# A fourth tile for the values of an attention stage, loaded at other places of the plan, and half the ring for GpSimd's transfers

## The chip, the cores and the metric

The kernel runs on one core of a Trainium2 chip. The metric is the device time of one execution in microseconds (us). A core has five engines with instruction streams of their own: TensorE (PE; its weight loads are shown apart as PEld), VectorE (DVE), ScalarE (ACT), GpSimd (POOL) and SyncE (SP). Each stream runs in order. SP computes nothing here: it issues nearly all transfers, and a transfer that has to wait holds everything behind it on SP. POOL issues some stores of the second half of the kernel.

## The reference, cut to what matters

Attention over 8 batches, 12 heads, 448 tokens and 64 elements per head, with the heads mixed by a 12x12 matrix before and another after the softmax; then a feed-forward layer on the 3584 x 768 result. Everything is float32.

```python
scores = scale * np.matmul(q, k.transpose(0, 1, 3, 2))
scores = np.einsum('bhij,hg->bgij', scores, w_pre)
scores = scores - np.max(scores, axis=-1, keepdims=True)
attn = np.exp(scores)
attn = attn / (np.sum(attn, axis=-1, keepdims=True) + 1e-09)
attn = np.einsum('bhij,hg->bgij', attn, w_post)
attn_out = np.matmul(attn, v)
# x: attn_out as [3584, 768]
h = x @ w_in            # 768 x 2048
g = h - np.tanh(h)
out = g @ w_out         # 2048 x 768
```

## The kernel before

**Two halves.** The attention stage takes the first 838 us or so of the span, the feed-forward stage the rest. [...]

**Blocks, groups, places.** Each batch has four blocks of query tokens (120, 120, 120 and 88). A block is cut into groups of ten tokens or fewer, so that ten tokens times twelve heads fill 120 partitions; a batch has 45 groups, all batches 360. Two groups make a *place*, the unit of the plan: 180 places (`NPL`), 22.5 to a batch. Place p does, in this order in the program:

- SP gathers the two groups of place p+2 (`gather`, L907: scores in SBUF, head-major, to rows of token and head, `t`), then sends what waits in two lists (`issue`, L769: at most six, the list of ordinary loads and stores ahead of the list of the weight conversion, each entry in a place after the one that asked for it);
- PE mixes the heads of place p (`premix`, L918, out of `t`, eight matmuls); DVE takes maxima (L927) and ACT exponentials (L929); DVE and POOL make the normalized second mixing matrix of place p-1 (`norm`, L936 to L938, `wr`);
- then come the jobs that the planner put at this place (`todo`): transposes of K (`prep_k`) and Q (`prep_q`), scores of a pair of heads for a later block (`scores`, L874), and attention times V for half the heads of an earlier block (`values`, L997);
- PE mixes place p-1 (`mix`, L955, 32 matmuls, needs `wr`), and DVE writes the result of `values` to a staging tile `x` (L1015). After every second block, and after the last of a batch, `x` is stored to DRAM (`xs`). There is one `x`, so the next write to it waits until that store has landed.

SP runs ahead of PE: what SP issues for place p goes out while PE is in p-1 or p, unless SP is held up.

**The weight conversion** (class `Convert`) runs through the attention stage as well: it loads a piece of the weights (`cr`), splits it on DVE, POOL and ACT, and stores the parts (`co` to `wi` or `wo`, `ct` to `ss` or `ts`). `co` has two buffers, so DVE's L88 and L94, which write into it, wait until an earlier store has landed. DVE being in order, all behind them waits too: `norm`, and so `mix` on PE.

**Values.** V of a batch comes in three loads of 448 KB (`load_v`, L784), hq = 0, 1, 2, each with four heads. The tag `vr` has three tiles, so load hq of batch b takes the tile of load hq of batch b-1. `values(i, 0)` reads loads 0 and 1, `values(i, 1)` reads 1 and 2. The loop at L1197 asks for load hq of batch b at place p0 + 4 + hq, where p0 is the first place of the batch; entries are sent in the next place. Loads of K (`load_k`, three per batch, 448 KB each in pieces of 256 B) and of Q (one per block) are asked for by the same planner.

**Names that the change touches:** `load_v` (L784) and its pool of tiles; the list `halved` and the loop that takes it apart (L1163 on), which fixes the place of each `values`; the loop at L1197; and the size of the ring at L1382.

Of the kernel before, what the change touches and what calls it, by code (L numbers as in the profile page):

```python
# [10 lines left out]
F32 = mybir.dt.float32  # L11
# [137 lines left out]
def kernel_body(  # L149
# [11 lines left out]
    nc = tc.nc  # L161
    B, H, S, D = q.shape
# [3 lines left out]
    NP = H // 2  # L166
    CP = 112
    NC = S // CP
# [567 lines left out]
    with ExitStack() as st:  # L736
# [7 lines left out]
        kp = st.enter_context(tc.tile_pool(name="kp", bufs=1, side="right"))  # L744
# [14 lines left out]
        def dma(dst, src, to=None):  # L759
            entry = [place[0], dst, src, None]  # L760
            (queue if to is None else to).append(entry)
            return lambda places=0: entry[3] is not None and entry[3] + places <= place[0]
# [19 lines left out]
            krs[b, hq] = t  # L782

        def load_v(b, hq):  # L784
            t = kp.tile([CP, 4, NC, D], F32, name="vr", tag="vr", bufs=3)
            sent[b, hq, "v"] = dma(
                t.rearrange("p h c d -> p h (c d)"),
                v[b, 4 * hq : 4 * hq + 4].rearrange("h (p c) d -> p h (c d)", c=NC),
            )
            vts[b, hq] = t  # L790
# [254 lines left out]
        for hq in range(3):  # L1045
            load_v(0, hq)
# [101 lines left out]
        def at_place(p, *job):  # L1148
            todo[p].append(job)

        halved = []
        for i in range(len(blocks)):
# [7 lines left out]
                    halved.append((e if i else x - 1, hi, "s", i + 1, x))  # L1160
            for x in range(2):
                halved.append(((f1 - 1) // 2 + 2, f2 // 2 + 1 if f2 < NG else NPL + 7, "v", i, x))
        at_s, p, kind = {}, 0, None  # L1163
        window = {i: (lo, hi) for lo, hi, k, i, _ in sorted(halved, reverse=True) if k == "s"}
        while halved:
            ready = sorted((x for x in halved if x[0] <= p), key=lambda x: (x[1], x[3:]))
            if ready:
                x = ready[0]
                assert p <= x[1], (p, x)

                other = [y for y in ready if y[2] != kind]
                if x[2] == kind and other and x[1] > p + 1:
                    x = other[0]
                halved.remove(x)
                _, _, kind, i, n = x
                if kind == "s":
                    at_s[i, n] = p
                    for hp in (2 * n, 2 * n + 1):
                        at_place(p, scores, i, hp)
                else:  # L1180
                    at_place(p, values, i, n)
            p += 1

# [2 lines left out]
        def held(p):  # L1186
            return [a for f, *a in todo[p] if f is scores]

        for p in range(1, NPL):
            if any(f in (scores, values) for f, *a in todo[p]):  # L1190
                continue
            for of, n in ((p - 1, 1), (p + 1, 0)):
                if len(held(of)) == 2 and window[held(of)[n][0]][0] <= p <= window[held(of)[n][0]][1]:
                    i, hp = held(of)[n]
# [4 lines left out]
        for i, (b, m) in enumerate(blocks):  # L1199
            p0 = first[i] // 2  # L1200
            if i + 2 < len(blocks):
                p = at_s[i + 2, 0] - 1
                at_place(p, prep_q, i + 2, 0)
                at_place(p, prep_q, i + 2, 1)
                if i + 3 < len(blocks):
                    at_place(p + 1, load_q, i + 3)
            if b and m == 0:
                for hq in range(NP // 2):
                    at_place(p0 + 4 + hq, load_v, b, hq)
        for b in range(1, B):  # L1210
            p, o, done = first[blocks.index((b - 1, 1))] // 2 - 4, 0, []
            for hq in range(3):
                if hq == 2:

                    p = max(p, done[0] + 1)
# [112 lines left out]
    for s in range(NS):  # L1328
# [24 lines left out]
        n = HELD[s] + AHEAD[s]  # L1353
# [44 lines left out]
```

## Time and profile before

| | |
|---|---|
| median of three runs | 1712.13 us (1706.76 to 1722.13) |
| the profiled execution, its own time | 1711.91 us |
| its span, first to last instruction | 1710.2 us |
| mean granted TensorE clock | 0.986 |
| busy share of the span: PE, PEld, DVE, ACT, POOL | 98%, 81%, 72%, 64%, 35% |
| instructions | 40889 |

The profile is of one execution. A busy PE is not PE at its peak, since matmuls overlap and their ends are modelled; what PE waits for is read from the waits, and how fast it ran from the granted clock (PEclk, 1.00 is full speed). A line of the timeline gives the start, the length, the engine, the line of the kernel, what is written and read, how many instructions were drawn together (x32), and in brackets the idle time of the engine before it with what ended it. A line of the windows gives a stretch, its length, the busy time and number of instructions of PE, PEld, DVE, ACT and POOL, then PEclk, the mean busy share of the 16 DMA engines, and GB/s.

### The profile page before, as it was taken

The page shows a single profiled execution, that of the slowest core. Times are in us where ns is not written, and L with a number is a line of the kernel's source. Part 1 is how long each engine was busy: PE and PEld are TensorE (multiplying, and loading weights), DVE is VectorE, ACT ScalarE, POOL GpSimd, SP SyncE. Part 2 cuts the span into 40 slices and gives each one's busy share as a digit, 9 for nine tenths or more (in the row PEclk, how much of TensorE's full clock was granted, in tenths as well). Part 3 has the DMA queues.
Part 4 walks back from the last instruction along what each step waited for, and adds up shares of the span by engine and source line. Part 5 has one row for each costly group of instructions (what it writes and reads, how often), then busy time and mean ns, then how long its engine had stood idle before and what let it go on. Part 6 is the DMA issues. An engine that isn't in the chain of part 4 may idle for free.

```text
span 1710.2 us, 40889 instructions
## 1 busy us (share of the span) xinstructions
PE 1668.2 (98%) x16068; PEld 1391.2 (81%) x16068; DVE 1238.5 (72%) x1939; ACT 1091.9 (64%) x1896; POOL 601.7 (35%) x798
## 2 busy tenths in 40 slices
PE   8999999999999999999999999999999999999999
PEld 6777777777777777777787888888888888889999
DVE  5776776868868788676488799858788868778432
ACT  4776776767767677677677677565667456665331
POOL 1566575666757667563100011101001101011100
PEclk9999999999999999999999999999999999999999
DMA  8779789787887988876579899988999989988993
GB/s 190 219 233 256 228 247 266 232 253 240 247 269 231 249 252 242 253 223 210 179 260 327 291 321 311 345 300 321 321 342 352 384 272 333 320 312 327 404 413 133
DMA packets 322286, 475.06 MB, mean 278 GB/s; under 512 B 105264, under 2 KB 255280, under 8 KB 322096
## 3 DMA queue, kind: packets, MB, share of 16 engines
q1 hardware_dynamic: 305660, 414.34, 74.9%
q0 software_dynamic: 16128, 57.68, 8.7%
q8 instruction: 128, 2.10, 0.5%
q14 instruction: 62, 0.51, 0.1%
q10 hardware_dynamic: 308, 0.43, 0.1%
HBM read 274.73 MB, written 120.59 MB: 231 GB/s over the span
## 4 chain that ended last, share of the span: by engine, by line
PE 82%; DMA 9%; DVE 4%; ACT 3%; issue 2%; SPq 1%; POOL 0%; ACTq 0%; DVEq 0%; POOLq 0%
PE ps_o L955 15%; PE ps_p L918 9%; PE ps_m L997 8%; PE ps_q L874 7%; PE ps_h L289 7%; PE ps_h L290 7%; PE ps_h L292 7%; PE y L530 6%; PE y L532 6%; PE y L531 6%; DMA gl<-gs 2%; DMA t<-s 2%; DMA vr<-in_v_dram 1%; PE ps_m L840 1%; DMA wi<-co 1%
## 5 line engine op out<-in xcount | busy, mean ns | idle before, releaser
L955 PEld LDWEIGHTS ps_o<-wr,e 60*112 60x112 f32 (+1 forms) x5760 | 310.1, 177 | 33.2 <-POOL wr L938 17.4
L955 PE MATMUL ps_o<-wr,e 60*112 60x60 f32 (+1 forms) x5760 | 317.8, 261 | 8.7 <-POOL wr L938 8.0
L929 ACT ACTIVATE e<-ps_p,mx 128x448 f32<-128x448 f32 x360 | 225.3, 631 | 114.6 <-DVE mx L927 76.2
L927 DVE TENSOR_REDUCE mx<-ps_p 128x1 f32<-128x448 f32 x360 | 206.6, 615 | 88.2 <-PE ps_p L918 87.7
L965 ACT COPY at<-ps_o 112x960 f32<-112x960 f32 x156 | 153.9, 986 | 116.1 <-PE ps_o L955 115.8
L918 PE MATMUL ps_p<-t,wpre 60*64 60x448 f32 (+1 forms) x1440 | 183.1, 576 | 9.5 <-DMA t<-s 7.6
L997 PEld LDWEIGHTS ps_m<-at,vr 112*64 112x64 f32 x3072 | 150.1, 138 | 29.6 <-issue 8.0
L997 PE MATMUL ps_m<-at,vr 112*64 112x120 f32 (+1 forms) x3072 | 164.3, 264 | 6.2 <-DMA vr<-in_v_dram 6.2
L938 POOL TENSOR_TENSOR wr<-wpost,zs 128x120 f32<-128x120 f32 x180 | 69.6, 387 | 286.4 <-DVE zs L937 221.2
L530 PE MATMUL y<-w,gh 128*128 128x384 f32 x448 | 151.1, 337 | 2.3 <-issue 0.8
L531 PE MATMUL y<-w,gh 128*128 128x384 f32 x448 | 150.3, 336 | 0.0
L532 PE MATMUL y<-w,gl 128*128 128x384 f32 x424 | 143.1, 337 | 2.0 <-DVE gl L448 2.0
L874 PEld LDWEIGHTS ps_q<-kk,qh 64*120 64x120 f32 (+1 forms) x768 | 60.4, 177 | 83.5 <-issue 43.0
L874 PE MATMUL ps_q<-kk,qh 64*120 64x448 f32 (+1 forms) x768 | 124.5, 401 | 1.2 <-DVE kk L826 0.5
L669 POOL DMA_DIRECT2D gs<-gb x24 | 17.2, 718 | 292.2 <-DVE gb L668 292.2
L879 DVE COPY s<-ps_q 120x448 f32<-120x448 f32 (+1 forms) x192 | 112.4, 614 | 8.7 <-PE ps_q L874 8.4
L305 ACT ACTIVATE u<-h 128x1024 f32<-128x1024 f32 x56 | 59.5, 1063 | 74.2 <-DVE h L716 70.2
L879 ACT COPY s<-ps_q 120x448 f32<-120x448 f32 (+1 forms) x192 | 95.0, 536 | 7.0 <-PE ps_q L874 6.7
L645 POOL DMA_DIRECT2D gs<-ga x24 | 17.2, 716 | 229.6 <-DVE ga L328 222.4
L530 PEld LDWEIGHTS y<-w,gh 128*128 128x128 f32 x448 | 84.1, 188 | 7.6 <-issue 2.1
L531 PEld LDWEIGHTS y<-w,gh 128*128 128x128 f32 x448 | 84.1, 188 | 3.4
L532 PEld LDWEIGHTS y<-w,gl 128*128 128x128 f32 x424 | 79.5, 188 | 3.0 <-DVE gl L448 3.0
(371 smaller groups left out, 3987.9 us busy)
## 6 DMA issues: line engine op xcount, KB each, us to landing
t<-s SPq DMA_DIRECT2D x342, 210.0 KB
wa<-ss SPq DMA_DIRECT2D x96, 384.0 KB
w<-wo SPq DMA_DIRECT2D x43, 768.0 KB
gl<-gs SPq DMA_DIRECT2D x62, 512.0 KB
wa<-wi SPq DMA_DIRECT2D x72, 384.0 KB
w<-ts SPq DMA_DIRECT2D x35, 768.0 KB
gs<-gs POOLq DMA_DIRECT2D x24, 768.0 KB, 9.1
cr<-in_moe_w_in_dram SPq DMA_DIRECT2D x48, 256.0 KB
```

Source lines behind the costliest of these rows:

```text
L289: nc.tensor.matmul(ph, w[:, c, 0], xh, start=start and c == 0, stop=False, skip_group_check=True)
L530: nc.tensor.matmul(y, gh[:, tok], wh, start=first, stop=False, skip_group_check=True)
L531: nc.tensor.matmul(y, gh[:, tok], wl, start=False, stop=False, skip_group_check=True)
L532: nc.tensor.matmul(y, gl[:, tok], wh, start=False, stop=last, skip_group_check=True)
L874: nc.tensor.matmul(ps[:n, :S], qx[a, hp, :], kx[a, hp % 2], start=(x == 0), stop=(x == 2))
L879: eng(sts[i][:n, 2 * hp + j, :], ps[:n, :S])
L918: nc.tensor.matmul(pss[r][halves[j], :], wpre[k, :], ts[j][k, :], start=True, stop=True)
L927: nc.vector.tensor_reduce(out=mx, in_=ps, axis=AX.X, op=ALU.max, negate=True)
L929: nc.scalar.activation(e, ps, AF.Exp, bias=mx, scale=1.0, accum_out=zs[:, 0, r : r + 1])
L955: nc.tensor.matmul(ps[:CP, j, c * GP : (c + 1) * GP].rearrange("p (h i) -> p h i", i=GI)[:, :, r * GH : (r + 1) * GH], e[k, c * CP : (c + ...
L965: nc.scalar.copy(ats[i0][:, :, :, at : at + 2 * GI].rearrange("p c h (j i) -> p j (c h) i", j=2), ps[:CP, :, : NC * GP].rearrange("p j (x ...
L997: nc.tensor.matmul(pv[j * D : (j + 1) * D, r, :n], vt[:, j, c, :], ats[i][:, c, 2 * hp + j, :n], start=(c == 0), stop=(c == NC - 1),)
```

## The change

Four tiles `vr` instead of three. The loads now take turns over four tiles: load hq of batch b takes the tile of the load four before it, so load 0 takes a tile whose last reader lies more than a batch back, load 1 that of load 0 of the batch before, load 2 that of load 1. Load 0 is asked for at p0 - 3, seven places sooner; load 1 at the place where `values(i-1, 0)` of the last block before stands, which is the last reader of its tile; load 2 at that of `values(i-1, 1)`. A dictionary `at_v` keeps these places. The ring for the descriptors of GpSimd's transfers shrinks from 4096 to 2048 bytes per partition; the fourth tile takes 4096.

```diff
         def load_v(b, hq):
-            t = kp.tile([CP, 4, NC, D], F32, name="vr", tag="vr", bufs=3)
+            t = kp.tile([CP, 4, NC, D], F32, name="vr", tag="vr", bufs=4)
...
-        at_s, p, kind = {}, 0, None
+        at_s, at_v, p, kind = {}, {}, 0, None
...
                 else:
+                    at_v[i, n] = p
                     at_place(p, values, i, n)
...
             if b and m == 0:
-                for hq in range(NP // 2):
-                    at_place(p0 + 4 + hq, load_v, b, hq)
+                at_place(p0 - 3, load_v, b, 0)
+                for hq in (1, 2):
+                    at_place(at_v[i - 1, hq - 1], load_v, b, hq)
...
-    nc = _bacc.Bacc("TRN2", target_bir_lowering=False, num_devices=1, dynamic_dma_scratch_size=4096)
+    nc = _bacc.Bacc("TRN2", target_bir_lowering=False, num_devices=1, dynamic_dma_scratch_size=2048)
```

Followed through the planner's arithmetic, the places at which the loads are asked for, and those of the first readers `values(i, 0)` and `values(i, 1)` of the batch, are:

| batch | loads 0, 1, 2 before | loads 0, 1, 2 after | first readers |
|---|---|---|---|
| 1 | 26, 27, 28 | 19, 24, 26 | 30, 32 |
| 2 | 49, 50, 51 | 42, 48, 50 | 52, 54 |
| 3 | 71, 72, 73 | 64, 69, 71 | 75, 77 |
| 4 | 94, 95, 96 | 87, 93, 95 | 97, 99 |
| 5 | 116, 117, 118 | 109, 114, 116 | 120, 122 |
| 6 | 139, 140, 141 | 132, 138, 140 | 142, 144 |
| 7 | 161, 162, 163 | 154, 159, 161 | 165, 167 |

The loads of batch 0, at the start of the kernel, stay where they are. No instruction is added and none is taken away.

## The prediction

> **What bounds the kernel now.** I read the page first: the busy shares and the chain of waits.
>
> ```profile
> PE 1668.2 (98%) x16068; PEld 1391.2 (81%) x16068; DVE 1238.5 (72%) x1939; ACT 1091.9 (64%) x1896; POOL 601.7 (35%) x798
> PE 82%; DMA 9%; DVE 4%; ACT 3%; issue 2%; SPq 1%; POOL 0%; ACTq 0%; DVEq 0%; POOLq 0%
> ```
>
> TensorE sets the end; transfers hold 9% of the chain. Whatever a load does, it is worth only the time for which PE stops or slows. Two of the longest waits of PE, then the issues of the values and two waits of VectorE, say where that is:
>
> ```profile
> PE ps_p L918 <- DMA t<-s: 7.6, 6, 2.7
> PE ps_m L997 <- DMA vr<-in_v_dram: 6.2, 3, 2.8
> ...
> L766 SPq DMA_DIRECT2D vr<-in_v_dram x24: 437/754/2998, 9.0 to 787.6; - x24
> DVE x L1015 <- DMA xs<-x: 8.1, 3, 3.3
> DVE co L88 <- DMA wi<-co: 13.6, 4, 6.1
> ```
>
> Columns of a wait: total us, times, longest. Of 24 loads of values only three stop PE, for 6.2 us in all. I looked for them in the timeline; here is batch 2 (places 52 and 53), with an undisturbed pair of places of the same work (58 and 59) below the first dots, and the stalls of batches 4 and 6 at the end:
>
> ```profile
> 259.82 0.98 PE L918 MATMUL ps_p<-t,wpre 60*64 60x448 f32 x8
> ...
> 265.32 1.04 PE L997 MATMUL ps_m<-at,vr 112*64 112x120 f32 x16 [1.76 <-DMA vr<-in_v_dram]
> 266.29 3.12 PE L955 MATMUL ps_o<-wr,e 60*112 60x60 f32 x32
> ...
> 275.00 0.98 PE L918 MATMUL ps_p<-t,wpre 60*64 60x448 f32 x8
> ...
> 291.13 0.98 PE L918 MATMUL ps_p<-t,wpre 60*64 60x448 f32 x8
> ...
> 297.29 0.98 PE L918 MATMUL ps_p<-t,wpre 60*64 60x448 f32 x8
> ...
> 299.49 1.69 PE L955 MATMUL ps_o<-wr,e 60*112 60x60 f32 x32
> ...
> 476.26 1.04 PE L997 MATMUL ps_m<-at,vr 112*64 112x120 f32 x16 [1.67 <-DMA vr<-in_v_dram]
> ...
> 687.62 1.04 PE L997 MATMUL ps_m<-at,vr 112*64 112x120 f32 x16 [2.76 <-DMA vr<-in_v_dram]
> ```
>
> The 32 matmuls behind the stall take 3.12 us, in an undisturbed place 1.69. So a stall costs more than its wait, and I measured whole stretches of places, from one premix to another, in the view by windows. The first three are the stalls of batches 2, 4 and 6, the fourth the undisturbed pair; then five places each at batches 1, 3 and 5 (29 to 33, 74 to 78, 119 to 123) and the five like them at batch 7 (164 to 168), undisturbed; the last is where load 0 of batch 2 will go.
>
> ```profile
> 259.82:275.00 15.18, 13.42 (x151) 10.30 (x149) 7.37 (x17) 7.15 (x16) 7.93 (x10) 0.78 0.94 278
> 470.90:485.94 15.04, 13.37 (x151) 10.23 (x149) 8.23 (x20) 7.65 (x17) 7.44 (x11) 0.77 0.97 299
> 681.17:697.30 16.13, 13.37 (x151) 10.23 (x149) 8.79 (x20) 7.08 (x16) 6.99 (x10) 0.79 0.96 273
> 291.13:301.11 9.98, 9.98 (x151) 7.88 (x149) 7.70 (x18) 7.60 (x18) 7.37 (x11) 1.00 0.86 301
> 150.53:181.01 30.48, 27.11 (x335) 20.48 (x333) 17.79 (x41) 15.69 (x37) 15.02 (x20) 0.83 0.85 248
> 363.00:391.84 28.84, 24.32 (x335) 18.22 (x333) 16.89 (x41) 17.09 (x40) 14.99 (x21) 0.94 0.92 269
> 573.48:601.86 28.38, 24.36 (x335) 18.40 (x333) 18.26 (x41) 16.33 (x38) 15.09 (x17) 0.94 0.91 250
> 783.97:806.15 22.18, 22.18 (x334) 17.52 (x333) 12.13 (x29) 14.46 (x36) 5.08 (x10) 1.00 0.71 230
> 219.32:229.19 9.87, 9.87 (x149) 7.87 (x147) 7.54 (x20) 6.80 (x16) 8.02 (x10) 1.00 0.57 200
> ```
>
> The numbers of PE's instructions agree within a group (151, 335 or 334), so lengths can be compared. Even batches lose 15.18 + 15.04 + 16.13 - 3 x 9.98 = 16.4 us, odd ones 30.48 + 28.84 + 28.38 - 3 x 22.18 = 21.2 us: 37.6 us in all. A loss is the wait plus the share of the clock that was not granted: in batch 2, 1.76 + 0.22 x 15.18 = 5.1 of 5.2 us. In all six the DMA engines are busy 85 to 97% of the time.
>
> [...]
>
> **The change part by part.** *Even batches.* PE waits at place 52 for load 1, which was sent in place 51 behind much else. It is now sent in place 49, load 0 in place 43, so both have landed and the three waits go. What is late next? SP's and VectorE's rows:
>
> ```profile
> 257.51 0.45 SPq L766 DMA_DIRECT2D vr<-in_v_dram  x1
> 258.06 0.70 SPq L766 DMA_DIRECT2D xs<-x  x1
> ...
> 267.29 0.79 DVE L1015 COPY x<-ps_m 128x360 f32<-128x360 f32 x1 [2.69 <-DMA xs<-x]
> ...
> 269.08 0.39 POOL L938 TENSOR_TENSOR wr<-wpost,zs 128x120 f32<-128x120 f32 x1 [4.32 <-DVE zs L937]
> ...
> 481.20 0.39 POOL L938 TENSOR_TENSOR wr<-wpost,zs 128x120 f32<-128x120 f32 x1 [4.38 <-DVE zs L937]
> ...
> 691.57 0.39 POOL L938 TENSOR_TENSOR wr<-wpost,zs 128x120 f32<-128x120 f32 x1 [5.68 <-DVE zs L937]
> ...
> 390.12 1.78 PE L955 MATMUL ps_o<-wr,e 60*112 60x60 f32 x32 [1.55 <-POOL wr L938]
> ```
>
> The store of `x` goes out right behind the load at 257.51, and VectorE can't write the next `x` before it lands at 267.29; `norm` queues behind that, `wr` is ready at 269.08 + 0.39 = 269.47, and `mix` needs it. Load 2 now takes the very position of load 1, so two loads still go out ahead of that store within three places. If it lands no earlier, PE reaches `mix` at 259.82 + 6.16 (291.13 to 297.29) + 2.20 (297.29 to 299.49) = 268.18 and waits 1.3 us; by the same steps 2.3 us at batch 4 (481.59 against 470.90 + 8.36) and 2.4 at batch 6 (691.96 against 681.17 + 8.36). That returns 16.4 - 6.0 = 10.4 us. Ends: 16.4 if the store is earlier, too; and 10.4 less 0.23 x 15.04 + 0.21 x 16.13 = 6.8 us, so 3.6, if the two waits over 1.67 us halve the clock as the old ones did (the wait of 1.55 us at 390.12 did not: the 32 matmuls behind it take 1.78 us, near the undisturbed 1.69). I take 10.4, between the ends.
>
> *Odd batches.* Here no load of values is waited for; they take up the DMA engines, and SP's time, while other things are late:
>
> ```profile
> 162.98 0.98 PE L918 MATMUL ps_p<-t,wpre 60*64 60x448 f32 x8 [2.75 <-DMA t<-s]
> ...
> 132.66 0.67 SPq L766 DMA_DIRECT2D kr<-in_k_dram  x1
> ...
> 154.68 1.63 SPq L907 DMA_DIRECT2D t<-s  x2
> ...
> 156.97 1.72 SPq L766 DMA_DIRECT2D wi<-co  x1
> ...
> 363.14 3.00 SPq L766 DMA_DIRECT2D vr<-in_v_dram  x1
> ```
>
> SP spent 3.00 us on the load at 363.14, against 0.45 at 257.51: it was held up by what was queued already. In batch 1 PE waits for the gather at 154.68; two loads of values are ahead of it before the change and, counted from 132.66 (place 25) on, two after it. Ahead of the store at 156.97, and of what corresponds to it in batches 3 and 5, it is three before and two after. A load is 458,752 B, at 278 GB/s 1.65 us. So by bytes one load per batch is out of the way, and the one that now goes out three places earlier may fit into time in which the engines were not full, another 1.65 us: 3 x 3.3 = 9.9 us at most by transfer time alone. Ends: 0, if all that is ahead of the gathers stays as late; 18, if the waits fall under what halves the clock and only some 1 us per batch is left. I take 8, near the 9.9, since batch 3's first wait has nothing less ahead of it.
>
> *The new positions.* Load 0 goes where the DMA share is 0.57 over 9.87 us: 4.2 us free for 1.65. Cost nothing; if that cover is gone, the gathers behind it are up to 1.65 us later, and they are issued two places ahead of their use. SP has one instruction more in those places and one less in the old ones.
>
> *The ring.* POOL's transfers are all in the second half:
>
> ```profile
> L670 POOL DMA_DIRECT2D gs<-gs x24: 750/760/778, 966.6 to 1583.4; - x24
> DMA to landing us min/median/max: 6.2/9.1/12.4
> ```
>
> POOL took 750 to 778 ns for each of the largest, so none waited for room. Cost taken: nothing. The rest of the second half is unchanged.
>
> Sum: 1711.9 (the profiled execution) - 10.4 - 8 = 1693.5 us, and the median before, 1712.1, is the same within 0.3.
>
> **The rivals.**
>
> *Next in line.* The waits move one step on and halve the clock again: 3.6 us from the even batches, some 2 from the odd: 1706. For it: the store and `wr` above, ready only 1.3 to 2.4 us after PE. Against it: at least one of three stays under 1.55 us without help.
>
> *The stalls go nearly whole.* Loads spread into free stretches end the congestion: 15 + 16 = 31 us, 1681. For it: batch 7 has the same places, with its loads of values at the old positions but no loads of K or of a next batch beside them, and no loss at 0.71 DMA share. Against it: the K loads stay where they are elsewhere.
>
> *Slower: SP held by the reader of the tile.* Loads 1 and 2 go out in the place after their tile's last reader, and SP runs ahead of PE. The closest:
>
> ```profile
> 130.29 1.97 PE ps_m L997 x48
> ```
>
> That reader ends at 132.26, and SP comes to the load at 132.66: 0.4 us to spare. If SP, with less ahead of it, arrives earlier, it stands up to 2 us, and two gathers, the store of `x` and conversion stores queue behind it, with PE behind the gathers. It decides where SP is early by more than what a gather has in hand; at a stall of batch 2's kind (5.2 us) for half of the 14 loads, 36 us more: 1694 + 36 = 1730. Against it: SP's gathers wait for PE's scores of the same place anyway.
>
> [...]
>
> **How the numbers follow.** A difference of about 1% (17 us) is what a measurement of this kernel can tell from no change. Chances: forecast 0.50 (13 to 24 us gained), next in line 0.27, nearly whole 0.16, SP held 0.05, the ring 0.02. Under 1695.0 lie the whole third case and two thirds of the forecast: faster 0.16 + 0.34 = 0.50. Within 1%: 0.16 + 0.27 = 0.43. Slower: 0.07. The range takes in the centres of the first three cases: 1680 to 1708; left out are the two slower cases (0.07) and some 0.06 at either side.
>
> **What would show it.** No wait of L997 for `vr`; PEclk 1.00 in places 52 and 53, 97 and 98, 142 and 143, and these pairs at 10 to 12.5 us. If they stay at 15 with PE waiting for `wr` or `t`, next in line is right. Batches 1, 3 and 5 at 24 to 29 us for five places, the third case at 22 to 24. SP waiting at L766 for PE's L997 would show SP held, POOL's issues over 0.8 us the ring. A change of the second half by more than 2 us would be outside all of these.

## The result, and the profile after

The changed kernel takes 1700.62 us (median of nine runs, 1694.30 to 1709.64); the kernel before took 1712.01 us beside it (nine runs, 1706.76 to 1722.13). The ratio is 0.9934, 95% interval 0.9914 to 0.9954: 11.4 us less, by the interval 7.9 to 14.7. That is a real gain, but under the 1% that the prediction named as a change. The forecast was 1693.5, a gain of 18.4 us. The profiled execution took 1702.33 us, its span is 1700.6, so the span is 9.6 us shorter than before.

The page of the changed kernel, busy time and the chain of waits (DMA was 9% of the chain, DVE 4%, ACT 3%):

```profile
PE 1661.3 (98%) x16068; PEld 1386.1 (82%) x16068; DVE 1238.2 (73%) x1939; ACT 1090.5 (64%) x1896; POOL 601.8 (35%) x798
PE 84%; DMA 8%; DVE 3%; ACT 2%; issue 1%; SPq 1%; POOL 0%; DVEq 0%; POOLq 0%; ACTq 0%
```

Its waits (total us, times, longest), PE's first, then two of VectorE:

```profile
PE ps_o L955 <- POOL wr L938: 9.2, 10, 3.4
PE ps_p L918 <- DMA t<-s: 9.2, 8, 2.7
...
PE ps_q L874 <- DVE x L1015: 1.6, 2, 0.9
...
DVE co L88 <- DMA wi<-co: 13.6, 6, 4.8
...
DVE x L1015 <- DMA xs<-x: 3.1, 2, 1.9
```

The wait of L997 for `vr` is gone. The wait for the gathers rose from 7.6 to 9.2 us, VectorE's wait for the store of `x` fell from 8.1 to 3.1, and its wait for the conversion's store is the same 13.6 us. New is a wait of PE behind the copy to `x` (L874).

The windows of the changed kernel: the pairs of places of batches 2, 4 and 6; the place right behind the pairs of batches 4 and 6 (99 and 144); the five places of batches 1, 3 and 5; the second half.

```profile
253.85:265.25 11.40, 10.53 (x150) 8.08 (x149) 7.46 (x17) 7.16 (x17) 7.79 (x10) 1.00 0.97 292
464.85:477.39 12.54, 10.71 (x148) 8.05 (x148) 7.14 (x17) 6.36 (x16) 5.37 (x8) 1.00 0.94 298
673.88:686.16 12.28, 10.74 (x151) 8.05 (x149) 7.41 (x16) 6.50 (x16) 6.16 (x7) 1.00 0.96 299
477.39:484.80 7.41, 7.41 (x96) 5.88 (x94) 5.12 (x12) 3.30 (x9) 4.59 (x6) 0.77 0.97 261
686.16:695.16 9.00, 9.00 (x96) 7.18 (x94) 5.23 (x13) 3.82 (x10) 4.92 (x7) 0.63 0.95 242
149.61:174.88 25.27, 22.64 (x334) 17.24 (x332) 18.14 (x41) 16.18 (x38) 15.43 (x21) 1.00 0.87 269
356.51:385.09 28.58, 25.20 (x333) 19.46 (x333) 15.78 (x38) 15.44 (x37) 14.14 (x20) 0.88 0.87 260
566.54:595.07 28.53, 25.38 (x335) 19.65 (x333) 17.05 (x40) 16.20 (x38) 14.57 (x17) 0.88 0.85 269
839.56:1700.60 861.04, 845.74 (x4370) 755.64 (x4368) 630.68 (x596) 504.09 (x578) 86.59 (x133) 1.00 0.89 319
```

The same of the kernel before for places 99 and 144 and for the second half, which the prediction had no need of:

```profile
485.94:491.78 5.84, 5.84 (x97) 4.81 (x95) 3.22 (x8) 2.88 (x7) 3.08 (x4) 1.00 0.82 248
697.30:703.14 5.84, 5.84 (x97) 4.81 (x95) 3.49 (x9) 3.47 (x8) 3.51 (x4) 1.00 0.95 243
847.48:1710.20 862.72, 847.13 (x4370) 756.87 (x4368) 630.51 (x596) 504.44 (x578) 86.35 (x133) 1.00 0.89 319
```

The three pairs gained 46.35 - 36.22 = 10.1 us, all at PEclk 1.00. But the place behind two of them now runs at 0.77 and 0.63 and gives back (7.41 - 5.84) + (9.00 - 5.84) = 4.7 us. The odd batches gained 30.48 + 28.84 + 28.38 - 25.27 - 28.58 - 28.53 = 5.3 us, nearly all of it in batch 1. The second half is 1.7 us shorter. In places between these stretches some 3 us were lost. What stands ahead of the lowered clock behind 477.39 is seen in the timeline of PE in the changed kernel:

```profile
473.89 0.47 PE L874 MATMUL ps_q<-kk,qh 64*120 64x448 f32 x2 [0.91 <-DVE x L1015]
...
475.68 1.78 PE L955 MATMUL ps_o<-wr,e 60*112 60x60 f32 x32 [0.92 <-POOL wr L938]
477.39 1.38 PE L918 MATMUL ps_p<-t,wpre 60*64 60x448 f32 x8
...
362.29 3.25 PE L955 MATMUL ps_o<-wr,e 60*112 60x60 f32 x32 [3.38 <-POOL wr L938]
...
573.87 1.77 PE L918 MATMUL ps_p<-t,wpre 60*64 60x448 f32 x8 [2.70 <-DMA t<-s]
```

Two waits of 0.91 and 0.92 us stand within 3 us of each other, and the eight matmuls behind them take 1.38 us instead of 0.98. The last two lines are the waits of batches 3 and 5, which are still there. SP and VectorE in the same kernel show what is behind the first and the third:

```profile
466.07 0.46 SPq L766 DMA_DIRECT2D vr<-in_v_dram  x1
466.63 1.33 SPq L766 DMA_DIRECT2D xs<-x  x1
...
473.06 0.78 DVE L1015 COPY x<-ps_m 128x360 f32<-128x360 f32 x1 [1.23 <-DMA xs<-x]
...
361.00 0.43 DVE L88 TENSOR_SCALAR co<-cr 128x512 int32<-128x512 int32 x1 [4.79 <-DMA wi<-co]
```

Load 2 goes out at 466.07, ahead of the store of `x`; that store lands late, VectorE stands for 1.23 us, and PE stands behind VectorE. In batch 3 VectorE stands 4.79 us at L88 for a store of the conversion.

### The profile page after: what moved, and what is told of

It reads as the page before. It is cut to its first block, busy times and chain, and to the rows that moved or that the text cites. A ratio compares the mean times of both kernels' runs of the same rounds, so it can differ in the third digit from the quotient of the medians.

```text
span 1700.6 us, 40900 instructions
## 1 busy us (share of the span) xinstructions
PE 1661.3 (98%) x16068; PEld 1386.1 (82%) x16068; DVE 1238.2 (73%) x1939; ACT 1090.5 (64%) x1896; POOL 601.8 (35%) x798
## 4 chain that ended last, share of the span: by engine, by line
PE 84%; DMA 8%; DVE 3%; ACT 2%; issue 1%; SPq 1%; POOL 0%; DVEq 0%; POOLq 0%; ACTq 0%
PE ps_o L955 15%; PE ps_p L918 9%; PE ps_m L997 9%; PE ps_h L289 7%; PE ps_h L292 7%; PE ps_h L290 7%; PE ps_q L874 7%; PE y L532 6%; PE y L530 6%; PE y L531 6%; DMA t<-s 3%; DMA gl<-gs 2%; PE ps_m L840 1%; PE ps_m L814 1%; DMA w<-wo 1%
## 5 line engine op out<-in xcount | busy, mean ns | idle before, releaser
L955 PEld LDWEIGHTS ps_o<-wr,e 60*112 60x112 f32 (+1 forms) x5760 | 305.8, 175 | 34.5 <-POOL wr L938 18.7
L955 PE MATMUL ps_o<-wr,e 60*112 60x60 f32 (+1 forms) x5760 | 314.1, 259 | 9.9 <-POOL wr L938 9.2
L927 DVE TENSOR_REDUCE mx<-ps_p 128x1 f32<-128x448 f32 x360 | 206.7, 616 | 80.8 <-PE ps_p L918 80.3
L997 PEld LDWEIGHTS ps_m<-at,vr 112*64 112x64 f32 x3072 | 153.1, 140 | 23.0 <-issue 8.5
L997 PE MATMUL ps_m<-at,vr 112*64 112x120 f32 (+1 forms) x3072 | 166.7, 266 | 0.0
L874 PEld LDWEIGHTS ps_q<-kk,qh 64*120 64x120 f32 (+1 forms) x768 | 58.8, 172 | 83.6 <-issue 42.3
L874 PE MATMUL ps_q<-kk,qh 64*120 64x448 f32 (+1 forms) x768 | 122.5, 393 | 2.8 <-DVE x L1015 1.6
```

Of the source, the lines that this page charges most:

```text
L874: nc.tensor.matmul(ps[:n, :S], qx[a, hp, :], kx[a, hp % 2], start=(x == 0), stop=(x == 2))
L927: nc.vector.tensor_reduce(out=mx, in_=ps, axis=AX.X, op=ALU.max, negate=True)
L955: nc.tensor.matmul(ps[:CP, j, c * GP : (c + 1) * GP].rearrange("p (h i) -> p h i", i=GI)[:, :, r * GH : (r + 1) * GH], e[k, c * CP : (c + ...
L997: nc.tensor.matmul(pv[j * D : (j + 1) * D, r, :n], vt[:, j, c, :], ats[i][:, c, 2 * hp + j, :n], start=(c == 0), stop=(c == NC - 1),)
```

## The experiments

All were compared with the kernel before on the same chip; the ratio weighs all executions and is not the ratio of the medians. Executions of one kernel differ by up to some 15 us (the two profiles of the changed kernel by 12.6 us in the attention stage alone), so the ratios rank the kernels, and a profile shows a mechanism in one execution. This table, whose lengths are worked out from the starts of the premixes in the timelines, goes with all that follows. "Odd" is the sum of the five places of batches 1, 3 and 5, "even" of the three places from 52, 97 and 142 on, "behind" of the places behind those (55 to 57, 100 to 105, 145 to 150); undisturbed they take 66.5, 47.9 and 62.7 us. The column "attention" runs from the premix of place 0 to that of place 179. The last is VectorE's total wait at L1015 that ended with the store of `x`; in batch 6 of the changed kernel another 2.97 us there are put down to PE. In the last two rows the lengths hold the fillers.

| kernel | median us | ratio | odd | even | behind | attention | wait for store of `x` |
|---|---|---|---|---|---|---|---|
| before | 1712.0 | 1 | 87.7 | 63.9 | 62.8 | 821.1 | 8.1 |
| ring_only | 1710.7 | 1.0013 | 84.4 | 57.8 | 66.2 | 815.2 | 6.3 |
| after | 1700.6 | 0.9934 | 82.4 | 58.5 | 64.4 | 813.3 | 3.1 |
| whole_again | 1699.9 | 0.9917 | 78.5 | 52.0 | 62.8 | 800.7 | 5.2 |
| load0_only | 1696.7 | 0.9922 | 79.4 | 48.1 | 71.2 | 805.8 | 0.7 |
| load0_again | 1699.8 | 0.9922 | 76.6 | 49.5 | 69.8 | 805.5 | 3.0 |
| loads12_only | 1715.7 | 1.0027 | 80.3 | 69.1 | 62.9 | 821.4 | 11.5 |
| loads01_only | 1693.4 | 0.9913 | 73.7 | 51.2 | 68.5 | 804.3 | none |
| store_first | 1693.7 | 0.9899 | 76.9 | 49.7 | 64.0 | 798.7 | 0.2 |
| store_first_again | 1694.5 | 0.9888 | 78.9 | 51.7 | 63.6 | 803.3 | none |
| load0_hold | 1692.5 | 0.9893 | 75.1 | 48.8 | 65.1 | 803.5 | 2.2 |
| store_first_hold | 1689.3 | 0.9857 | 73.3 | 52.8 | 65.7 | 802.8 | 2.6 |
| filled_waits | 1695.4 | 0.9913 | 77.7 | 53.9 | 63.0 | 803.2 | 5.9 |
| load0_filled | 1696.7 | 0.9914 | 80.3 | 49.6 | 67.5 | 804.6 | 2.5 |

**The ring alone.** The kernel before, with the smaller ring:

```diff
-    nc = _bacc.Bacc("TRN2", target_bir_lowering=False, num_devices=1, dynamic_dma_scratch_size=4096)
+    nc = _bacc.Bacc("TRN2", target_bir_lowering=False, num_devices=1, dynamic_dma_scratch_size=2048)
```

> The kernel before with the ring at 2048 bytes and nothing else changed. Theory (the ring costs nothing, since POOL issued every one of its stores in 750 to 778 ns before and the largest landed within 12.4 us): the time stays within 3 us of the kernel before, 1712 us. Rival (the smaller ring takes back part of what the loads bring): 5 to 10 us slower, with POOL's largest issues over 0.8 us.

Measured: 0.9992 to 1.0033. POOL's issues, in the view by line of this kernel, take what they took before (750/760/778 ns):

```profile
L670 POOL DMA_DIRECT2D gs<-gs x24: 750/760/778, 961.2 to 1578.8; - x24
```

The ring costs nothing and brings nothing.

**Load 0 alone.** Four tiles, load 0 at its new place, loads 1 and 2 at their old ones (difference to the changed kernel):

```diff
                 for hq in (1, 2):
-                    at_place(at_v[i - 1, hq - 1], load_v, b, hq)
+                    at_place(p0 + 4 + hq, load_v, b, hq)
```

> Four tiles and the small ring; only load 0 of each batch is asked for seven places sooner, loads 1 and 2 stay at p0+5 and p0+6. Theory A (PE waits for load 1, so load 1 has to go out sooner): the waits of values for their load shrink by at most one load's 1.65 us but two of three remain, the even stretches stay near 14 us, and the time is 3 to 5 us under the kernel before. Rival B (what counts is the number of bytes in the crowded places, whichever load it is): taking load 0 out is enough, the waits of 1.67 to 2.76 us fall under what halves the clock, and the time is 9 to 13 us under the kernel before, as with the whole change.

Measured: 0.9922, 0.9893 to 0.9951, a median 12.3 us under the kernel before, as rival B had it. The whole gain is there. The windows of this kernel, places 97 to 99 and then 55 to 57:

```profile
467.15:483.00 15.85, 15.85 (x244) 12.85 (x243) 11.28 (x24) 10.44 (x24) 10.41 (x13) 1.00 0.96 285
...
272.36:287.57 15.21, 13.65 (x146) 9.60 (x144) 9.99 (x26) 9.15 (x21) 8.18 (x11) 0.78 0.81 244
```

The even stretch runs undisturbed at a DMA share of 0.96. But a wait has moved on: places 55 to 57 take 15.21 us where 10.2 is undisturbed, and the timeline has one wait of PE there:

```profile
275.66 2.98 PE L955 MATMUL ps_o<-wr,e 60*112 60x60 f32 x32 [1.55 <-POOL wr L938]
```

A wait of 1.55 us, and the matmuls behind it run at half speed. The wait of the same 1.55 us that the prediction took as harmless was followed by 1.78 us. The profiles show one difference between the two. In the clock records of all fourteen, each change of the granted clock lies a whole multiple of 3.413 us from the first one. So the time of an execution can be cut into intervals of that length, and these are the windows of load0_only, then of the kernel before, along them:

```profile
272.58:275.99 3.41, 1.85 (x20) 0.71 (x14) 3.34 (x9) 1.74 (x3) 1.40 (x4) 1.00 0.89 264
275.99:279.41 3.42, 3.42 (x38) 2.77 (x36) 1.00 (x4) 2.18 (x6) 1.83 (x3) 0.50 0.91 315
...
385.93:389.35 3.42, 2.65 (x34) 1.41 (x32) 2.53 (x6) 2.55 (x6) 2.04 (x5) 1.00 0.95 304
389.35:392.76 3.41, 2.64 (x42) 1.87 (x42) 2.08 (x6) 2.56 (x6) 1.11 (x3) 1.00 0.87 285
392.76:396.17 3.41, 3.41 (x52) 2.52 (x50) 3.28 (x5) 2.72 (x7) 2.84 (x3) 1.00 0.90 207
```

In load0_only the whole 1.55 us lie in one interval, and the next one runs at 0.50. In the kernel before the boundary at 389.35 cuts the wait in two, 0.77 and 0.78 us, and the clock stays at 1.00, in the interval behind these two as well. The interval alone does not decide: the one that ends at 695.8 in load0_only was idle for 1.60 us, and no fall followed.

**Loads 1 and 2 alone.** Load 0 back at its old place, the other two at their new ones:

```diff
-                at_place(p0 - 3, load_v, b, 0)
+                at_place(p0 + 4, load_v, b, 0)
```

> Four tiles and the small ring; load 0 stays at p0+4, loads 1 and 2 are asked for where the whole change asks for them. Theory A: load 1 is landed when it is needed, its waits are gone, and most of the gain is here, 6 to 10 us under the kernel before; load 0, now between loads 1 and 2 and needed first, is the new risk at the even batches. Rival B (bytes in the crowded places): nothing has left them, the gain is under 3 us, and PE waits for load 0 in place of load 1.

Measured: 1.0027, 1.0005 to 1.0049, a little slower than before. Now all three loads go out ahead of the store of `x`. Places 97 to 99 (47.9/3 = 16 us undisturbed) and the timeline of PE inside them:

```profile
465.42:489.66 24.24, 19.68 (x242) 15.11 (x243) 12.35 (x28) 10.04 (x23) 10.31 (x14) 0.86 0.92 275
```

```profile
468.41 2.68 PE L997 MATMUL ps_m<-at,vr 112*64 112x120 f32 x48 [1.10 <-DMA vr<-in_v_dram]
...
477.26 0.47 PE L874 MATMUL ps_q<-kk,qh 64*120 64x448 f32 x2 [2.54 <-DVE x L1015]
...
479.05 3.25 PE L955 MATMUL ps_o<-wr,e 60*112 60x60 f32 x32 [0.92 <-POOL wr L938]
```

PE waits less for values (1.3 us in all, 6.2 before) and more for VectorE, which waits for the store of `x`. So load 0 out of the way is worth the gain, and loads 1 and 2 sooner are worth nothing by themselves: what they gain at L997, the later store takes back.

**Work for PE in its waits.** The changed kernel with matmuls of the identity ahead of some premixes and mixes; they write a tile that the next real matmul overwrites, so they add PE work and nothing else:

```diff
+        FILL_P = {31: 5, 74: 7, 97: 3, 120: 12}
+        FILL_M = {52: 2, 73: 15, 97: 4, 142: 4}
...
+            for _ in range(FILL_P.get(p, 0)):
+                nc.tensor.matmul(pss[1][:, :P], ident, ident, start=True, stop=True)
...
+            for _ in range(FILL_M.get(p, 0)):
+                nc.tensor.matmul(ps[:, 0, :P], ident, ident, start=True, stop=True)
```

> The changed kernel with idle matmuls of the identity (0.21 us each) put on PE where the changed kernel's PE waited: 5, 7, 3 and 12 ahead of the premix of places 31, 74, 97 and 120; 2, 15, 4 and 4 ahead of the mix of 52, 73, 97 and 142. They compute nothing that is kept. Theory (the four losses of the clock in the changed kernel, 3.4 to 6.8 us at half speed each and 23.9 us in all, come from PE's idle time just ahead of them): the granted clock stays 1.00 through the attention stage and the time falls by 5 to 12 us under the changed kernel's 1700.6, to 1689 to 1696. Rival (the clock falls for another cause, or the waits alone cost the time): the clock falls as before and the time is the same or up to 5 us longer.

Measured: 1695.40 us, 0.9913, 0.9884 to 0.9942. The mean clock of the profiled execution is 0.998 (0.991 after). Places 97 to 99 and 142 to 144 by windows, and the timeline at the place of the two short waits (the mix is L961 in this kernel, the fillers L956, the copy L1021):

```profile
462.39:480.75 18.36, 17.58 (x252) 13.83 (x251) 11.82 (x26) 9.45 (x23) 9.86 (x12) 1.00 0.95 289
...
666.89:685.23 18.34, 17.57 (x252) 13.83 (x250) 12.15 (x26) 10.32 (x24) 11.10 (x13) 1.00 0.96 266
```

```profile
471.30 0.66 PE L874 MATMUL ps_q<-kk,qh 64*120 64x448 f32 x3 [0.78 <-DVE x L1021]
...
472.10 1.16 PE L956 MATMUL ps_o<-ident 128*128 128x128 f32 x8
473.19 1.78 PE L961 MATMUL ps_o<-wr,e 60*112 60x60 f32 x32
474.90 0.98 PE L922 MATMUL ps_p<-t,wpre 60*64 60x448 f32 x8
```

The first wait is still there, the second is filled, and the premix behind takes its full-speed 0.98 us. Places 97 to 99 and 142 to 144 take 18.4 and 18.3 us where the changed kernel took 20.0 and 21.3. That fits idle time of PE, in pieces under 1 us, as the cause there. One profile does not show it, since an execution of the changed kernel without fillers (whole_again, below) kept its clock in these places too (PEclk 1.00 in both). As a whole the interval overlaps that of the change; the gain over it is not shown.

**Load 2 behind the store of `x`.** The changed kernel, with load 2 asked for in the same place but entered behind the store:

```diff
-                for hq in (1, 2):
-                    at_place(at_v[i - 1, hq - 1], load_v, b, hq)
+                at_place(at_v[i - 1, 0], load_v, b, 1)
+                at_place(at_v[i - 1, 1], lambda *to: last.append(partial(load_v, *to)), b, 2)
```

> The whole change, except that load 2, asked for in the same place as before, stands in SP's queue behind the store of x of that place and not ahead of it. Theory C (loads 1 and 2 sooner put 448 KB ahead of the store of x, on which VectorE and then mix wait): VectorE's wait for that store falls from 1.9 and 1.2 us to under 0.5, the three even places-triples (52 to 54, 97 to 99, 142 to 144) fall from 17.2, 20.0 and 21.3 us towards the quiet 16.0, and the time is 14 to 18 us under the kernel before, 4 to 6 under the whole change. Rival D (it is the number of bytes in the crowded places ahead of the gathers, not the one store): only the store gains, the triples stay at 17 to 20, and the time is that of the whole change, 10 to 12 us under the kernel before.

Measured: 0.9899, 0.9871 to 0.9928. SP and PE in the timeline, at the places shown of the changed kernel:

```profile
460.59 0.58 SPq L766 DMA_DIRECT2D xs<-x  x1
461.27 0.60 SPq L766 DMA_DIRECT2D vr<-in_v_dram  x1
...
469.65 1.78 PE L955 MATMUL ps_o<-wr,e 60*112 60x60 f32 x32 [0.92 <-POOL wr L938]
471.36 0.98 PE L918 MATMUL ps_p<-t,wpre 60*64 60x448 f32 x8
```

The same bytes in the other order: VectorE's wait for the store goes (0.2 us in all, against 3.1), PE's wait behind it goes too, the second wait is the same 0.92 us, and the clock stays whole (PEclk 1.00 over places 97 to 99, 460.16 to 477.20). With two neighbours on SP swapped, the 1.23 us wait at L1015 shrank to 0.2 us at most.

**Loads 0 and 1.** Load 2 back at its old place, which is behind the store as well:

```diff
+                at_place(at_v[i - 1, 0], load_v, b, 1)
+                at_place(p0 + 6, load_v, b, 2)
```

> Four tiles and the small ring; loads 0 and 1 as in the whole change, load 2 back at p0+6, behind the store of x and the gathers of its place. Theory C (load 2 ahead of the store is what took the gain of load 0 back): as good as load 0 alone, 12 to 15 us under the kernel before, even triples at 16 to 17 us. Rival D' (load 1 sent two or three places sooner is what hurts, as it is what stands ahead of the gathers of the next places): between the whole change and loads 1 and 2 alone, 3 to 9 us under the kernel before.

Measured: 0.9913, 0.9880 to 0.9946. No wait at L1015. By the ratio it is 14.9 us under the kernel before, as theory C had it, and above the 3 to 9 us of rival D'. It stands between load0_only and store_first and can't be told from either.

**The conversion held back, with load 0 alone.** In twelve places the conversion's step is left to a later place when it would start with L88; no work is left out:

```diff
+        HOLD = {30, 31, 32, 54, 55, 56, 76, 77, 78, 119, 120, 121}
...
-                if p not in short:
+                if p not in short and not (p in HOLD and any(x[1] == 1 for x in conv.active)):
                     conv.step()
```

> Load 0 alone sooner, and the step of the weight conversion that waits for its own earlier store (L88 on VectorE) is not run at places 30 to 32, 54 to 56, 76 to 78 and 119 to 121, but after them. Theory E (what is left at the odd batches is VectorE, in order, standing at L88 ahead of the normalization that PE's mix needs): the five places at batches 1, 3 and 5 fall from 26.9, 27.7 and 24.8 us to 23 to 25, and the time is 4 to 8 us under load 0 alone. Rival F (the wait is of the full DMA engines and moves to the gathers or to another step): the same time within 3 us, with PE waiting for t.

Measured: 0.9893, 0.9864 to 0.9922. VectorE's waits at L88 for `wi` fall from 13.6 to 0.9 us, those for `wo` rise from 6.2 to 8.8 us. The five places of batches 1, 3 and 5 take 24.8, 26.4 and 23.9 us (23 to 25 expected), odd plus behind falls from 150.6 to 140.2 us. But a wait appears where there had been none: places 165 to 168, 18.2 us in load0_only, by windows run at

```profile
763.35:786.91 23.56, 21.40 (x283) 16.58 (x281) 13.01 (x30) 12.94 (x31) 13.06 (x16) 0.86 0.66 209
```

behind this instruction of VectorE in the timeline:

```profile
767.86 0.43 DVE L88 TENSOR_SCALAR co<-cr 128x512 int32<-128x512 int32 x1 [4.71 <-DMA wo<-co]
```

The work put off meets its own stores later. About half of the wait at L88 has gone, the rest has moved; the interval overlaps that of load0_only, so a gain over it is not shown.

**Fillers, with load 0 alone.** Fillers as above, at the places where load0_only had waited:

```diff
+        FILL_P = {31: 4, 77: 8, 103: 6, 147: 6}
+        FILL_M = {30: 7, 54: 6}
```

> Load 0 alone sooner, and idle matmuls of the identity (0.21 us each) on PE where its profile showed waits: 4, 8, 6 and 6 ahead of the premix of places 31, 77, 103 and 147; 7 and 6 ahead of the mix of places 30 and 54. They compute nothing that is kept. Its profile lost 3.4, 6.8 and 6.8 us at half clock, 8.5 us of work. Theory: the clock stays 1.00 through the attention stage and the time is 4 to 8 us under load 0 alone, the best so far. Rival (the places of the waits differ from execution to execution, so matmuls put where one profile showed them miss half of them and cost their own time): within 3 us of load 0 alone.

Measured: 1696.74 us, 0.9914, 0.9888 to 0.9941: no better than load0_only. The waits came elsewhere: in its timeline PE waits 1.52 us in batch 5, at a place without fillers, and the premix behind takes 1.77 us:

```profile
571.26 2.38 PE L961 MATMUL ps_o<-wr,e 60*112 60x60 f32 x32 [1.52 <-POOL wr L942]
573.57 1.77 PE L922 MATMUL ps_p<-t,wpre 60*64 60x448 f32 x8
```

**The three versions again, on one chip, and both measures together.** The first three are unchanged; the last adds to store_first the hold, in places chosen from its own waits:

```diff
+        HOLD = {30, 31, 32, 54, 55, 56, 73, 74, 75, 97, 98, 99, 119, 120, 121}
```

> The changed kernel itself, on one chip with the next three and the kernel before. Expected from the first measurement: 10 to 13 us under the kernel before.

> Load 0 alone sooner, once more, beside the whole change. Theory C (loads 1 and 2 sooner give nothing and, with load 2 ahead of the store of x, take some back): as fast as the whole change or up to 5 us faster, 12 to 17 us under the kernel before. Were the earlier difference chance, it would be the slower of the two by some us.

> The whole change with load 2 behind the store of x in SP's queue, once more, beside the whole change. Theory C: 4 to 8 us faster than the whole change, 15 to 19 us under the kernel before, the even triples at 16 to 17 us. Were the earlier difference chance: within 2 us of the whole change.

> Load 2 behind the store of x, and the conversion's step L88 not run at places 30 to 32, 54 to 56, 73 to 75, 97 to 99 and 119 to 121 but after them. If the two effects add: 20 to 26 us under the kernel before, the fastest here, the five places at batches 1, 3 and 5 at 22.5 to 25 us. If what is left at the odd batches is the full DMA engines and not VectorE's order: within 3 us of the run before, with PE waiting for t, or a new wait at batch 7, where the shifted conversion then falls (places 163 to 168).

Measured beside 1714.03 us for the kernel before: the whole change 1699.94 (0.9887 to 0.9947), load 0 alone 1699.83 (0.9893 to 0.9951), the store first 1694.47 (0.9859 to 0.9918), the store first with the hold 1689.31 (0.9825 to 0.9889). So load 0 alone equals the whole change (first runs 0.9922 and 0.9934). The store first is 5.5 us under the whole change here and was ahead in the first runs too (0.9899); the intervals overlap, the direction is the same both times. In its second profile the three places of batch 4 take 18.8 us, not the 16 to 17 expected: PE waits 1.70 us ahead of a premix there, and that premix takes 1.77 us, where 0.98 is undisturbed. With the hold it is the fastest kernel of this study, 24.7 us under the kernel before and 10.6 under the change, and its interval just touches that of the change; it overlaps that of the store first, so the gain of the hold alone is not shown. Its waits at L88 for `wi` are down from 12.7 us (store_first):

```profile
DVE co L88 <- DMA wi<-co: 3.2, 2, 1.7
```

and the five places of batch 3, which no other version brought under 25 us, are nearly undisturbed in its windows (23.10 against 22.18 us):

```profile
355.71:378.81 23.10, 22.09 (x335) 17.37 (x333) 14.89 (x37) 15.24 (x36) 11.19 (x15) 1.00 0.81 243
```

The rest of this profile is no better than store_first's: batch 5 still takes 26.8 us (22.5 to 25 expected), with PE waiting 2.38 us for a gather, the three places of batch 2 take 20.4 us, where VectorE waits 2.60 us for the store of `x` although it goes out first, and the attention stage is as long (802.8 us against 798.7 and 803.3). So where the shorter median comes from is not shown.

The second profile of the whole change shows how far one execution goes. Places 97 to 99 by windows, and the only wait of PE in them with the premix behind it, from the timeline:

```profile
461.28:478.78 17.50, 16.55 (x244) 12.86 (x242) 11.74 (x26) 10.34 (x24) 10.48 (x13) 1.00 0.93 284
```

```profile
471.22 1.78 PE L955 MATMUL ps_o<-wr,e 60*112 60x60 f32 x32 [0.92 <-POOL wr L938]
472.94 0.98 PE L918 MATMUL ps_p<-t,wpre 60*64 60x448 f32 x8
```

The same kernel, without PE's wait behind the copy to `x` in this execution, though VectorE waited 1.89 us for the store there: one wait of 0.92 us, and the clock does not fall (PEclk 1.00). This execution took 1692.25 us, the shortest of its six.

## Why the prediction was right or wrong

*The three waits for `vr` go, the cost of each is wait plus clock:* right. L997 no longer waits for `vr` in the changed kernel, and the three pairs gained 10.1 us where 10.4 were forecast, at PEclk 1.00, within the 10 to 12.5 us named (12.54 for the longest). That the size fits is in part luck. The forecast left 6.0 us in the pairs, all of it waits for `wr`; 6.3 us were left, of which 2.3 are waits for `wr`, 1.6 waits behind the copy to `x`, 0.3 other idle time, and 2.0 a longer busy time of PE.

*What is late next:* the right rows, `wr` behind the store of `x`; the waits for `wr` were 0.5, 0.9 and 0.8 us in batches 2, 4 and 6, where 1.3, 2.3 and 2.4 us were forecast.

*What the residual waits cost:* wrong, and this is the step of the prediction that failed. It let a wait under 1.55 us cost itself alone, from one row, and asked only whether a single wait was long enough. Behind two waits of 0.91 and 0.92 us PEclk was 0.77, behind those of batch 6 it was 0.63: 4.7 us back out of 10.1. With one of the two filled (filled_waits), gone by the order of two transfers (store_first), or absent in another execution of the same kernel (whole_again), the clock stayed whole at that very place (PEclk 1.00 in all three). That the two waits add up is not shown: the boundary at 474.43 parts them, the interval with the first, 0.91 us idle, was not followed by a fall, the one with the second, 0.92 us idle, was. What the runs show in place of the length of one wait is the idle time in an interval of 3.413 us. From 33 to 840 us, the fourteen profiles hold 3232 such intervals at full clock and 53 falls. All 27 intervals with more than 1.61 us of PE idle time were followed by a fall, none with less than 0.9 us was, and of the 67 between 26 were. That is the "next in line" rival in part: the waits moved on and halved the clock, but in the place behind the pair, for which the sum has no term.

*"Load 2 now takes the very position of load 1", taken as neutral:* wrong in what it overlooked. It keeps two loads ahead of the store of `x`, and VectorE waits for that store. With three loads ahead of that store VectorE waited 11.5 us for it, with two (the four profiles of before, ring_only and the whole change) 3.1 to 8.1, with one (load 0 alone, store first) 0 to 3.0. The prediction credited the change as a whole; its gain comes from load 0 (0.9922 twice, against 1.0027 for loads 1 and 2), and loads 1 and 2 sooner bring nothing that can be measured until the store goes first. What they bring then, 0.9899 and 0.9888, has intervals that overlap those of load 0 alone.

*Odd batches, 8 us:* mis-sized in this profile, 5.3 us; the second profile gives 87.7 - 78.5 = 9.2. The mechanism is argued from the order of the transfers and fits only in part. Batch 1, where the gather has less ahead of it, gained 5.2 us. Batch 3 gained 0.3 us; the prediction had said that its first wait has "nothing less ahead of it", and its long wait is now that behind L88. Batch 5 still waits 2.70 us for a gather.

*The rivals:* the stalls did not go nearly whole in any version; the stretches still stand at a DMA share of 0.85 to 0.97. SP was not held by the tile's reader: its longest issue of a load of values took 1875 ns by the view by line, where before it was 2998. The ring cost nothing, as taken: 1.0013 (0.9992 to 1.0033) with the ring alone, with POOL's largest issues at 750 to 778 ns as before; no run shows a loss behind its 0.02.

*New positions at no cost:* right as far as seen; places 40 to 44, where load 0 of batch 2 goes out, take the 21.3 us they took before. *Second half:* 1.7 us, under the 2 us named.

*The sum:* against the profiled execution, 1702.33 - 1693.5 = 8.8 us too long: 4.7 for the two places at a lowered clock and 0.3 at the pairs, 2.7 in the odd term, 2.9 lost between the stretches (821.1 - 813.3 = 7.8 gained in the attention stage, where odd and even alone make 10.7), less 1.7 in the second half. The direction was right and the size too large. The 11.4 us between the medians lie under the 13 to 24 us of the forecast's own case and above the 6 us or so of "next in line"; the outcome is the one named "within 1%", which had 0.43. That 1% was too coarse a measure: nine executions each gave 0.2% to either side. In an execution in which the clock held behind the pairs (whole_again) the attention stage is 20.4 us shorter than before, a little over the 18.4 forecast; the median of its six is not.

*What stays open:* why PE still waits for a gather at batch 5 in store_first_hold, with no wait at L88 there, and what decides in the intervals with 0.9 to 1.61 us of idle time. The 26 of them that were followed by a fall hold 1.60 us of `mix` on average, the 41 others 0.38; that is a correlation, and no run tested it.

## What to carry to other kernels

On a queue that is kept full, ask of each moved load what it goes ahead of: here one transfer whose landing an engine waited for was a store, and with it sent first the median fell by 5.5 us beyond the 14.1 of the whole change, with intervals that overlap. Test the parts alone: one of three moved loads carried the gain. And when you ask whether PE's clock will fall, add up its idle time over each interval of the clock record, here 3.413 us, where all 27 intervals with more than 1.61 us were followed by a fall, rather than go by the length of one wait. Which part of a wait lies in which interval differs between executions, so one profile is not enough.

## What the runs showed of the hardware

The granted clock of TensorE was 1.00 or 0.50 in every record, and in each of the fourteen profiles it changed only at multiples of 3.413 us from its first change. In the attention stage a fall followed every interval at full clock with more than 1.61 us of idle time, and none with less than 0.9 us. So a gap of 1.55 us in one interval was followed by half clock (275.99 in load0_only), and one of 1.55 us cut by a boundary into 0.77 and 0.78 us was not (390.12 before), nor one of 2.05 us cut into 1.32 and 0.73 us (474.37 in ring_only). No interval had to be idle from end to end for a fall: the one ahead of the fall at 477.84 in the changed kernel was idle for 0.92 of its 3.41 us. No run here moved a gap against these intervals on purpose.
